# Transposed weight loads in quarters of 1024 columns, and TensorE transposes with filler products at the end of a two-layer recurrent kernel

## The chip, the cores and the metric

The kernel runs on one NeuronCore of a Trainium2 chip. The metric is the device time of one execution in microseconds (us). The engines are TensorE (PE, with its weight loads as PEld), VectorE (DVE), ScalarE (ACT), GpSimd (POOL) and SyncE (SP). SP does no arithmetic here; it issues nearly all DMAs, in program order.

## The reference

A block A (attention in segments, with a carried memory) and a gated block B (GLU) are applied in turn, twice, with the same weights and a layer norm in front of each. All data are bf16.

```python
# x: [1, 2048, 448]; 16 heads of 256; segments of 32 tokens; 8 memory rows
def A(x, mem, Wq, Wk, Wv, Wo):
    for s in range(64):
        h = concat([mem, x[32*s : 32*s+32]])          # 40 rows
        q, k, v = h @ Wq, h @ Wk, h @ Wv              # per head, 448 -> 256
        p = softmax(where(mask, q @ k.T / 16, -1e9))
        o = sum over heads of (p @ v) @ Wo            # 40 x 448
        mem = o[:8]                                   # next segment waits for this
        outs.append(o[8:])
    return concat(outs)
def B(x):                                             # F = 1792
    return (relu(x @ Wg) * (x @ Wu)) @ Wd
x = x + A(ln(x), mem0); x = x + B(ln(x))
x = x + A(ln(x), mem0); x = x + B(ln(x))
```

## The kernel before

**Folded weights.** The kernel first makes, per head, M = Wq Wk^T and N = Wv Wo, both with 448 rows and columns, and keeps them in SBUF (`M`, `M3`, `N`). For this `setup` needs Wq, Wk and Wv with the head dimension on the partitions, so it loads them by transposing DMAs from HBM (`load_t`, issued on SP at line 537), while Wo comes by plain DMAs (`load_o`, line 541). Wq, Wk and Wv are [448, 4096] each; one `load_t` of before moves 2048 columns, that is 1.835 MB, so there are six of them: Wq0, Wk0, Wq1, Wk1, then Wv0, and after two plain loads of Wo (0.92 MB each) Wv1. Then the products: for each of 16 heads three products of two accumulation steps plus a packed fourth for the last 64 rows. The products of four heads (a quarter) are 32 PE instructions, for M as for N, and each result is copied out of PSUM by ACT (line 706) or DVE (line 707). A product waits for the semaphore of the whole DMA that brings its operand: in before, the first eight heads of M wait for Wq0 and Wk0, the other eight for Wq1 and Wk1.

**Steps.** 68 steps `step(t)` follow. Step t works on segment t of layer 0 and on segment t-4 of layer 1. `t_block` forms h M for all heads, `s_mem`, `p_t_mem`, `u_mem`, `un_mem` and `m_t` carry the memory on to the next step, and `s_seg`, `seg_pt`, `u_seg` do the 32 tokens. Two steps make a tile p: `un(p)` multiplies the weighted rows by N (56 pieces), `ln_b(p)` normalizes, `b_layer(p)` is the GLU. In the last step (t = 67) `un(33)`, `ln_b(33)`, `b_layer(33)`, `ln_b(34)` and `b_layer(34)` are called; `b_layer(34)` works on rows that `un(33)` makes, so nothing else is left to run beside the way from `un(33)` to `b_layer(34)`.

**Transposes inside a step.** `seg_pt` turns the softmax weights (`Ps` to `PTs`) and `ln_b` the normalized rows (`xn` to `xBT`) by transposing DMAs from SBUF to SBUF (`tdma`, on SP, line 768). `p_t_mem` turns the small memory part on PE, with the identity matrix as one operand.

**Order of the work.** Operations are recorded with a cost and their reads and writes; `_Order.run` then schedules them on the engines by these costs, due times and the constants of `BIAS`, and hands out the eight PSUM banks (`tile("R", 1)`). The result is a fixed order on each engine; an instruction that waits holds up all that stands behind it on the same engine. In the built program the order of the six `load_t`, four `load_o` and the first two `xAT` transposes (the normalized input rows of the first tiles, from `ln_a`) on SP is: Wq0, Wk0, Wq1, Wk1, Wv0, Wo0, Wo1, Wv1, Wo2, Wo3, xAT, xAT.

Of the kernel before, what the change touches and what calls it, by code (L numbers as in the profile page):

```python
# [6 lines left out]
BF = dt.bfloat16  # L7
# [22 lines left out]
NP = (NSEG + LAG) // 2  # L30
NSTEP = NSEG + LAG
# [346 lines left out]
def MM(out, lhsT, rhs, **kw):  # L378
    return (out, lhsT, rhs, kw)


class _Kernel:
# [131 lines left out]
    def setup(self):  # L514


        S = self
        NW = S.N[:, :, :].rearrange("p o d -> p (o d)")
        BG = S.big[:, :]
        W8 = 8 * D  # L520
# [9 lines left out]
        st = {k: v.rearrange("p (k d) -> p k d", k=8) for k, v in place.items()}  # L530
        src = {"Wq": S.Wq_d, "Wk": S.Wk_d, "Wv": S.Wv_d}

        def load_t(w, i):

            both = {"Wq": NW[:, 4 * i * W8:(4 * i + 2) * W8], "Wk": NW[:, 2 * W8:4 * W8] if i == 0 else BG[:, 0:2 * W8],
                    "Wv": BG[:, (2 * i + 2) * W8:(2 * i + 4) * W8]}[w].rearrange("p (k d) -> p k d", k=16)
            S.q.add("dma", ("sp",), {"sp": 5300.0}, lambda E: E.dma_start_transpose(out=both, in_=src[w][:, i * 2048:(i + 1) * 2048]),
                    (), [(w, 2 * i), (w, 2 * i + 1)], name=f"{w}{i}", lat=2500.0)

        def load_o(q, wr=()):  # L540
            S.q.add("dma", ("sp",), {"sp": 3000.0}, lambda E: E.dma_start(st["Wo", q], S.Wo_d[:, q * 8:q * 8 + 8, :]),
                    (), [("Wo", q)] + list(wr), name=f"Wo{q}", lat=2500.0)
# [1 line left out]
        def small(name, fn, wr, lat=4000.0):  # L544
            S.q.add("dma", ("act",), {"act": 120.0}, fn, (), wr, name=name, lat=lat)

        for i in range(2):
            load_t("Wq", i)
            load_t("Wk", i)
        for p in range(2):  # L550
            S.load_x(p, small)
        small("m0", lambda E: E.dma_start(S.mNc[0:MEM, 0:D], S.mem_d), [("mNc", 0)])
# [35 lines left out]
        T = S.tile("R", 1)  # L588
# [15 lines left out]
        for i in range(H // 2):  # L604
            q = i // 2
            for odd in range(2):
                u = i + 8 * odd
                for kt in range(3):
                    T = S.tile("R", 1)
# [6 lines left out]
            T = S.tile("R", 1)  # L616
            S.mm(lambda T=T, i=i: pair3("Wq", "Wk", i, T), 2 * S.pitch(D), [("Wq", q), ("Wk", q)], T.res() + [("stage",)], mode=6)
            for odd in range(2):
                u, r = i + 8 * odd, slice(64 * odd, 64 * odd + 64)
                for c in range(4):  # L620
                    side, slot = S.PLACE[16 * c + (u if c < 3 else i)]
                    d, w, x = 64 * side, (128 if c < 3 else 64), (64 * odd if c == 3 else 0)
# [4 lines left out]
        S.Nkeys = [("N", o) for o in range(NO)]  # L627

        for q in range(4):
            if q % 2 == 0:  # L630
                load_t("Wv", q // 2)
            load_o(q, [("Wk", q)] if q > 1 else [])
        def n_main(q):
            for h in range(4 * q, 4 * q + 4):
# [126 lines left out]
    def ln_b(self, p):  # L761
        S = self
        S.ln(S.XB[:, p % 2, :], [("XB", p % 2, i) for i in range(3)], 16, "lnB", 1)
        S.tdma("xBT", lambda: S.xBT[:, :, :], lambda: S.xn[:, 1, :], [("xn", 1, 0), ("xn", 1, 1)], [("xBT",)])

    def tdma(self, name, out, src, rd, wr):

        self.q.add("dma", ("sp",), {"sp": 1250.0}, lambda E: E.dma_start_transpose(out=out(), in_=src()), rd, wr, name=name, lat=1150.0)
# [131 lines left out]

    def seg_pt(self, t):
        S = self
        S.tdma("pts", lambda: S.PTs[:, :].rearrange("p (a x) -> p a x", a=4), lambda: S.Ps[:, :, :].rearrange("p a x -> p (a x)"),
               [("Ps",)], [("PTs",)])

# [138 lines left out]
    def un(self, p):  # L1044
        S = self
        O = S.tile("R", 1)
        XA = lambda r, q: S.XA[r, q % 4, :]
        XB = lambda r, q: S.XB[r, q % 2, :]
        lo, x, y = slice(0, 64), slice(64, 96), slice(96, 128)
        if p % 2 and LAG // 2 < p < NSEG // 2:  # L1050

            for k in range(0, NO, 2):
                S.mm(lambda k=k: [MM(O.b()[:, 0:D], S.U[:, o, :], S.N[:, o, :], start=(o == 0), stop=(o == NO - 1)) for o in (k, k + 1)],
                     2 * S.pitch(D), [("U", i, k // 16) for i in range(4)], O.res())
            for src, q, dst, g, half in ((lo, p, lo, p, 0), (x, p - 1, y, p, 1), (y, p, y, p + 1, 1)):
                S.dve(lambda E, src=src, q=q, dst=dst, g=g: E.tensor_tensor(XB(dst, g), O.b()[src, 0:D], XA(dst, q), ALU.add), D,  # L1056
                      O.res(half=(half,)) + [("XA", q % 4, half)], [("XB", g % 2, 2 * half)])
        else:

            u = (2, 3) if p == NSEG // 2 else (0, 1)  # L1060
            for k in range(0, NO, 4):
                S.mm(lambda k=k: [MM(O.b()[64 * (o % 2):64 * (o % 2) + 64, 0:D], S.U[:, o, 32 * u[0]:32 * u[0] + 64], S.N[:, o, :], start=(o < 2), stop=(o >= NO - 2))
                                  for o in range(k, k + 4)], 2 * S.pitch(D), [("U", i, k // 16) for i in u], O.res(), mode=6)
            if p < NSEG // 2:
                S.halves(O, XB(lo, p), XA(lo, p), [("XA", p % 4, 0)], lo, [("XB", p % 2, 0)])
            elif p == NSEG // 2:
                S.halves(O, XB(y, p + 1), XA(y, p), [("XA", p % 4, 1)], y, [("XB", (p + 1) % 2, 2)], 32)
            else:
                r = slice(64, 128)
                S.halves(O, XB(r, p + 1), XA(r, p), [("XA", p % 4, 1)], r, [("XB", (p + 1) % 2, i) for i in (1, 2)])  # L1070
        S.load_x(p + 4)

    def b_layer(self, p):
# [114 lines left out]
```

## Time and profile before

| | us |
|---|---|
| median of 7 runs | 1629.07 |
| lowest, highest | 1624.81, 1632.05 |
| profiled execution, its own time | 1629.28 |
| span of the profile (first to last instruction) | 1627.5 |
| PE busy | 1547.3 (95%) |
| DVE busy | 1070.6 (66%) |
| ACT busy | 718.7 (44%) |
| DMA landing: PTs from Ps, xBT from xn (median) | 2.4, 2.6 |
| mean granted TensorE clock | 0.992 |

The profiled execution took 1.8 us more than its span. It lies 0.2 us above the median. In a line of a timeline the columns are start, duration, engine, source line, operation, output and input, and the count; a bracket at the end gives the idle time of the engine just before and what ended it. In a table of windows PE and PEld are followed by busy us and the number of instructions, and PEclk is the granted clock as a share of full speed.

### The profile page before, as it was taken

To read this page: it belongs to the slowest core of one execution; us is meant where nothing else is said; L and a number is where in the kernel's file an instruction comes from. 1 tells how busy PE (TensorE), PEld (TensorE's weight loads), DVE (VectorE), ACT (ScalarE), POOL (GpSimd) and SP (SyncE) were. 2 spreads that over 40 slices of the span, in tenths; PEclk is the share of its full clock that TensorE was granted. 3 is DMA by queue.
4 is the path that set the end of the run, shared out by engine and by line. 5 is a ranking of instruction groups with operands and counts; after the bars stand their busy time and mean duration, and the time that the engine had idled before them with its cause. 6 is when DMAs were issued, how large, how long until landed. Compare 5 with 4: busy or idle time off the path is not lost. (4 is left out here: it accounts for less than half of the span.)

```text
span 1627.5 us, 67481 instructions
## 1 busy us (share of the span) xinstructions
PE 1547.3 (95%) x30194; PEld 1117.5 (69%) x30194; DVE 1070.6 (66%) x2988; ACT 718.7 (44%) x2163; POOL 90.7 (6%) x156
## 2 busy tenths in 40 slices
PE   4989999999999999999999999999999999999996
PEld 2556767777766776777667776776677777766675
DVE  7746666667666766666666766666667666667554
ACT  4624444445343444444344444444344444534332
POOL 3100000000000000000000000000000000000000
PEclk9989999999999999999999999999999999999999
DMA  9620000000000000000000000000000000000010
GB/s 233 189 84 19 16 14 19 19 15 18 15 19 13 19 16 18 18 14 16 18 16 17 16 19 18 14 15 18 15 17 16 19 19 14 18 13 14 17 21 16
DMA packets 130096, 45.46 MB, mean 28 GB/s; under 512 B 118920, under 2 KB 128912, under 8 KB 129808
## 3 DMA queue, kind: packets, MB, share of 16 engines
q1 hardware_dynamic: 129456, 40.92, 11.4%
q8 instruction: 238, 3.90, 1.0%
q10 hardware_dynamic: 352, 0.24, 0.1%
q14 instruction: 50, 0.41, 0.1%
HBM read 10.33 MB, written 1.84 MB: 7 GB/s over the span
## 5 line engine op out<-in xcount | busy, mean ns | idle before, releaser
L128 PE MATMUL b<-hT,Mw 128*128 128x80 bf16 (+1 forms) x11424 | 440.8, 200 | 12.8 <-DVE big L707 7.3
L128 PEld LDWEIGHTS b<-hT,Mw 128*128 128x128 bf16 x11424 | 418.5, 100 | 35.5 <-DVE big L707 13.3
L128 PE MATMUL b<-Nw,big 128*64 128x448 bf16 (+1 forms) x1936 | 307.7, 356 | 1.4 <-ACT Nw L706 0.7
L128 PE MATMUL b<-xBT,big 128*128 128x128 bf16 (+1 forms) x3920 | 217.9, 217 | 10.0 <-DMA xBT<-xn 10.0
L128 PEld LDWEIGHTS b<-xBT,big 128*128 128x128 bf16 x3920 | 208.0, 99 | 11.6 <-DMA xBT<-xn 11.3
L707 DVE CAST TTs<-b 128x320 bf16<-128x320 f32 (+5 forms) x423 | 192.1, 454 | 32.5 <-PE b L128 31.5
L706 ACT ACTIVATE TTs<-b 64x256 bf16<-64x256 f32 (+4 forms) x461 | 191.7, 416 | 38.9 <-PE b L128 30.8
L128 PEld LDWEIGHTS b<-Nw,big 128*64 128x64 bf16 (+1 forms) x1936 | 126.8, 104 | 111.1 <-issue 19.3
L128 PE MATMUL b<-Nw,UTm 128*32 128x448 bf16 x3752 | 192.3, 356 | 1.4 <-ACT UTm L706 1.3
L706 ACT ACTIVATE TTm<-b 128x80 bf16<-128x80 f32 (+5 forms) x400 | 91.6, 229 | 226.7 <-PE b L128 225.7
L707 DVE CAST TTm<-b 128x80 bf16<-128x80 f32 (+5 forms) x484 | 111.8, 231 | 112.1 <-PE b L128 106.7
L128 PEld LDWEIGHTS b<-Nw,UTm 128*32 128x32 bf16 x3752 | 97.8, 97 | 90.2 <-issue 19.3
L707 POOL COPY hK<-xn 32x448 bf16<-32x448 bf16 x136 | 75.7, 556 | 1462.3 <-DVE xn L743 1456.0
L128 PE MATMUL b<-hT,M 64*128 64x80 bf16 (+3 forms) x3808 | 139.9, 197 | 8.1 <-DVE TTs L707 3.7
L707 DVE CAST big<-b 128x512 bf16<-128x512 f32 (+1 forms) x163 | 107.2, 675 | 58.9 <-PE b L128 57.8
L1090 ACT ACTIVATE gT<-b 128x256 bf16<-128x256 f32 x227 | 85.5, 379 | 106.6 <-PE b L128 81.3
L707 DVE CAST UTm<-b 128x448 bf16<-128x448 f32 (+2 forms) x107 | 64.8, 615 | 101.6 <-PE b L128 100.3
L128 PEld LDWEIGHTS b<-hT,M 64*128 64x128 bf16 (+1 forms) x3808 | 105.7, 97 | 24.3 <-DVE hT L707 10.1
L1091 DVE TENSOR_TENSOR hB<-gT,b 128x256 bf16<-128x256 bf16 x227 | 90.6, 411 | 44.2 <-ACT gT L1090 39.2
L706 ACT ACTIVATE big<-b 128x512 bf16<-128x512 f32 (+1 forms) x225 | 106.4, 514 | 8.1 <-PE b L128 7.0
L950 ACT ACTIVATE hi<-b 128x448 bf16<-128x448 f32 x67 | 36.4, 543 | 146.3 <-PE b L128 144.5
L706 ACT ACTIVATE UTm<-b 128x448 bf16<-128x448 f32 (+2 forms) x144 | 76.3, 552 | 39.5 <-PE b L128 37.6
(100 smaller groups left out, 1520.2 us busy)
## 6 DMA issues: line engine op xcount, KB each, us to landing
big<-in_A_Wo_dram SPq DMA_DIRECT2D x3, 896.0 KB, 5.8
out_dram<-ys SPq DMA_DIRECT2D x32, 56.0 KB, 1.9
big<-in_B_W_down_dram SPq DMA_DIRECT2D x1, 1568.0 KB, 6.9
XA<-in_A_x_dram SPq DMA_DIRECT2D x28, 56.0 KB, 2.2
big<-in_B_W_up_dram SPq DMA_DIRECT2D x1, 1344.0 KB, 5.8
big<-in_B_W_gate_dram SPq DMA_DIRECT2D x1, 1344.0 KB, 8.6
PTs<-Ps SPq DMA_TRANSPOSE x68, 2.4
Nw<-in_A_Wo_dram SPq DMA_DIRECT2D x1, 896.0 KB, 7.5
```

The source lines that it names most:

```text
L128: ins = E.matmul(out, lhsT=lhsT, rhs=rhs, **kw)
L706: return E.activation(out(), src(), ACT.Copy)
L707: return E.tensor_copy(out(), src())
L950: S.act(lambda E: E.activation(S.hi[:, :], C.b()[:, 0:D], ACT.Copy), D, C.res(), [("hi",)])
L1090: S.act(lambda E, k=k, R=R, n=n: E.activation(S.gT[:, k % 2, 0:n], R[0].b()[:, 0:n], ACT.Relu), n, R[0].res(), [("gT", k % 2)])
L1091: S.dve(lambda E, k=k, R=R, n=n, fcs=fcs: E.tensor_tensor(S.hB[:, fcs[0]:fcs[-1] + 1, 0:w], S.gT[:, k % 2, 0:n].rearrange("p (a b) -> p a ...
```

## The change

`load_t` moves 1024 columns (0.92 MB) at a time, so there are twelve of them. SP's order in the built program becomes: Wq0, Wk0, Wq1, Wk1, Wq2, Wk2, Wq3, Wk3, Wv0, Wo0, Wv1, Wo1, Wv2, Wo2, Wv3, Wo3, xAT, the first load of W_up, xAT. A quarter of M or N now waits for the DMAs of its own quarter. On PE the third quarter of N (32 instructions, and two of the fourth) now stands in front of the first `t_block` of step 0, where in before about half of N stood between and behind the parts of that block.

In step 67 `seg_pt` transposes with four PE instructions (`pe_transpose`) and one copy out of PSUM; the built program puts the copy on DVE, between the GLU's products. `ln_b(34)` does the same; its copy is on ACT. After the two additions of `un(33)` that read its PSUM bank, `warm` issues eight products of 512 columns, whose result nobody reads. On PE the order at the end becomes: GLU 33 (112 products, the four transposes of `Ps` after the first 64), weighted rows (5), 2 products of W_down, `un(33)` (56), 12 products of W_down, 8 filler products, 4 transposes of `xn`, GLU 34 (112 and 14). In before, 6 products of W_down stood ahead of `un(33)` and 8 behind it. The instructions of steps 1 to 66 keep their order on every engine.

```diff
-        def load_t(w, i):
-            both = {"Wq": NW[:, 4 * i * W8:(4 * i + 2) * W8], "Wk": NW[:, 2 * W8:4 * W8] if i == 0 else BG[:, 0:2 * W8],
-                    "Wv": BG[:, (2 * i + 2) * W8:(2 * i + 4) * W8]}[w].rearrange("p (k d) -> p k d", k=16)
-            S.q.add("dma", ("sp",), {"sp": 5300.0}, lambda E: E.dma_start_transpose(out=both, in_=src[w][:, i * 2048:(i + 1) * 2048]),
-                    (), [(w, 2 * i), (w, 2 * i + 1)], name=f"{w}{i}", lat=2500.0)
+        def load_t(w, q):
+            S.q.add("dma", ("sp",), {"sp": 3600.0}, lambda E: E.dma_start_transpose(out=st[w, q], in_=src[w][:, q * 1024:(q + 1) * 1024]),
+                    (), [(w, q)], name=f"{w}{q}", lat=2500.0)
...
-        for i in range(2):
-            load_t("Wq", i)
-            load_t("Wk", i)
+        for q in range(4):
+            load_t("Wq", q)
+            load_t("Wk", q)
...
         for q in range(4):
-            if q % 2 == 0:
-                load_t("Wv", q // 2)
+            load_t("Wv", q)
             load_o(q, [("Wk", q)] if q > 1 else [])
...
     def ln_b(self, p):
         S = self
         S.ln(S.XB[:, p % 2, :], [("XB", p % 2, i) for i in range(3)], 16, "lnB", 1)
+        if p == NP:
+            T = S.pe_transpose([("xn", 1, 0), ("xn", 1, 1)], lambda a: S.xn[:, 1, a * 128:a * 128 + 128], [("xBT",)])
+            S.cp(lambda: S.xBT[:, :, :].rearrange("p a b -> p (a b)"), lambda: T.b().bitcast(BF)[:, 0:512], 512, T.res(), [("xBT",)])
+            return
         S.tdma("xBT", lambda: S.xBT[:, :, :], lambda: S.xn[:, 1, :], [("xn", 1, 0), ("xn", 1, 1)], [("xBT",)])
+
+    def pe_transpose(self, rd, src, wr):
+        S = self
+        T = S.tile("R", 1)
+        S.mm(lambda: [MM(T.b().bitcast(BF)[:, a * 128:a * 128 + 128], src(a), S.ident[:, :], is_transpose=True) for a in range(4)],
+             4 * S.pitch(128), rd + [("ident",)], T.res() + wr)
+        return T
+
+    def warm(self, n, rd, wr):
+        S = self
+        T = S.tile("R", 1)
+        S.mm(lambda: [MM(T.b()[:, 0:512], S.ident[:, :], S.N[:, 0:2, 0:256], start=True, stop=True) for _ in range(n)], n * S.pitch(512), rd, T.res() + wr)
...
     def seg_pt(self, t):
         S = self
+        if t == NSTEP - 1:
+            T = S.pe_transpose([("Ps",)], lambda a: S.Ps[:, a, :], [("PTs",)])
+            S.cp(lambda: S.PTs[:, :], lambda: T.b().bitcast(BF)[:, 0:512], 512, T.res(), [("PTs",)])
+            return
         S.tdma("pts", ...)
...
                 S.halves(O, XB(r, p + 1), XA(r, p), [("XA", p % 4, 1)], r, [("XB", (p + 1) % 2, i) for i in (1, 2)])
+                S.warm(8, O.res(), [])
```

## The prediction

> **What bounds the kernel.** I read the page's busy shares first (PE 95%), then the chain of waits, then the timelines of the two ends, since the diff touches only these. Steps 1 to 66 keep their order on all engines, so what an end gains or loses goes whole into the time.
>
> The chain's end:
>
> ```profile
> 1611.16 0.63 DVE part L1041
> ...
> 1613.79 0.19 DVE stat L737
> ...
> 1614.66 0.62 DVE xn L743 x2
> 1615.28 0.02 issue
> 1615.30 2.39 DMA xBT<-xn
> 1617.68 0.05 issue
> 1617.73 6.10 PE b L128 x126
> ```
>
> From the end of `un(33)` at 1611.1 all is serial: two additions, the norm, the transpose by DMA (2.39 us), GLU 34. The granted clock by windows:
>
> ```profile
> 1596.30:1599.00 2.70, 0.70 (x17) 0.56 (x17) 1.84 (x10) 0.67 (x4) 0.00 (x0) 1.00 0.26 55
> ...
> 1600.50:1602.00 1.50, 1.50 (x33) 1.50 (x31) 0.42 (x1) 0.18 (x2) 0.00 (x0) 0.50 0.43 87
> ...
> 1612.00:1617.70 5.70, 0.00 (x0) 0.00 (x0) 3.11 (x7) 0.50 (x2) 0.00 (x0) 0.94 0.15 33
> 1617.70:1619.00 1.30, 1.27 (x24) 1.27 (x25) 0.00 (x0) 0.00 (x0) 0.00 (x0) 0.50 0.00 0
> ...
> 1620.50:1622.30 1.80, 1.80 (x66) 1.75 (x62) 0.48 (x2) 0.75 (x2) 0.00 (x0) 1.00 0.00 0
> ```
>
> After 5.86 us without PE work GLU 34 starts at half clock (0.50), and only from about 1620.3 runs at 1.00.
>
> The beginning, SP's timeline, PE's first products, and the wait at the end of the loads:
>
> ```profile
> 0.74 7.74 SPq L537 DMA_TRANSPOSE Nw<-in_A_Wq_dram  x1
> 8.54 7.79 SPq L537 DMA_TRANSPOSE Nw<-in_A_Wk_dram  x1
> 16.37 7.84 SPq L537 DMA_TRANSPOSE Nw<-in_A_Wq_dram  x1
> 24.26 7.70 SPq L537 DMA_TRANSPOSE big<-in_A_Wk_dram  x1
> ```
> ```profile
> 18.63 13.67 PE L128 MATMUL b<-Nw 128*128 128x448 bf16 x64 [11.40 <-DMA Nw<-in_A_Wk_dram]
> 34.62 11.56 PE L128 MATMUL b<-big,Nw 128*128 128x448 bf16 x64 [2.31 <-issue]
> ...
> 60.49 0.51 PE L128 MATMUL b<-hT,M 64*128 64x40 bf16 x20 [2.57 <-DVE hT L707]
> ```
>
> PE starts when Wk0 is there (18.5), waits 2.31 us for Wk1, and at 57.9 has done all that stands ahead of `t_block`, while xAT, behind ten loads in SP's queue, lands only at 60.2. So the setup ends by the queue, not by its beginning. The DMA rates from 10 to 30 us, in slices of 0.25 us:
>
> ```profile
> GB/s 135 142 178 151 289 278 291 290 289 292 289 288 292 293 287 292 291 290 288 292 291 289 291 292 289 289 292 291 286 294 291 176 85 99 165 289 284 290 257 167
> GB/s 123 0 1 121 267 292 288 290 294 289 287 293 290 290 289 295 288 288 322 271 240 77 8 7 181 277 291 292 288 291 291 159 143 18 146 274 294 289 288 292
> ```
>
> A transpose streams at 290 GB/s, which is 6.33 us for 1.835 MB, yet one is issued every 7.8 us. The 1.45 us between show as dips: about 0.55 us at 17.75, where Wk0 ends and Wq1 begins, then about 0.9, 0.8 and 0.6 us at 19.5, 25 and 28, within 2 us of a data start or end.
>
> **Part 1, the loads.** Six transposes become twelve of half the size. The trace shows no HBM transpose of 1024 columns. Bounds for what each of the six further ones adds: nothing, if the dips go with the bytes; 1.45 us, if all go with the instruction. I take 0.75, a little over the one dip that lies cleanly between two instructions (0.55): 4.5 us. Transposes and copies also alternate more: two more changes from transpose to copy; the rates dip for about 0.6 us at such a change (40.5 to 41.25), so 1.2 us (0 to 1.2). xAT then lands 5.7 us later (0 to 9.9), at 65.9 instead of 60.2. Everything behind it on SP (the loads of W_up, W_down, W_gate, the second xAT) shifts along; these wait for PE's reads of the old weights anyway.
>
> Against this, PE gets its first quarter after two issues of about 4.3 us, half of 7.8 + 0.75, in place of two of 7.8, some 7 us sooner, and M and three quarters of N are done by the time xAT lands. In before, from xAT's use at 60.49 to the product of the memory rows with N at 79.67, PE did half of N (64 instructions) beside `t_block`; now 32 of these lie in front. They are worth 5.5 us: 24 at the pace of N's start (26 in 4.56 us) and 8 in 0.95 us. Setup: 5.7 - 5.5 = +0.2 us; ends -5.5 and +4.4. The moved evictions on DVE and ACT lie beside these products, and both engines idle in the same stretch.
>
> The skill's page "DMA: Bandwidth & Descriptors", section Bandwidth, speaks against this part: it wants DMAs of at least 1 MiB, and a quarter is 0.875 MiB. A line through its rows for 1 MB (6.15 us) and 16 MB (79.0 us) leaves 1.3 us per DMA, an estimate for plain loads; with it the setup would come to +3.5 us in place of +0.2.
>
> **Part 2, the last GLU tile.** *Transpose.* 2.44 us from xn to the first product go. In their place: four PE transposes, 0.23 us for one (`p_t_mem`, at 1582.15) and 0.06 for each further one (128-column products, 32 in 1.95 us), 0.41; the copy of 512 columns on ACT, 0.51 us (mean of that form on line 706); three hand-offs of 0.05. Together 1.07: gain 1.37 us. Bounds: at half clock and with 0.6 for the copy the gain is 0.9.
>
> *Clock.* The eight fillers wait for both additions (1612.4) and PE has 12 products of W_down until about 1612.2. A 512-column product takes about 0.23 us (14 of 448 columns in 2.82 us), so they end at 1614.2, and PE idles 1.0 us until xn and 0.6 us during the copy. The nearest rows: 2.31 us of idle after dense work left the clock at 1.00 (34.6), while 0.8 and 1.3 us with 0.7 us of work between brought 0.50 (1599). Two shorter gaps with 2.2 us of work around them lie nearer to the first, so I take the clock as held. GLU 34's 112 products then go at 27.3 ns (66 in 1.80 us), 3.06 us in place of 4.63: gain 1.57, or 0 if it drops. The fillers stand ahead of nothing but the transposes, which xn releases later.
>
> The skill's page "TensorE: Matmul & The Clock Gate" allows idle gaps up to about 3 us, which would hold the clock, but says in Part 4 that transposes do not count as work. The row at 1599, a drop after gaps of 0.8 and 1.3 us, is stricter than the first rule.
>
> *`seg_pt`.* The DMA of PTs issued at 1599.78 lands 2.4 us later, but PE uses it only at 1604.47: hidden, gains nothing. Its four transposes add 0.3 us to PE ahead of `un(33)` (0.25 to 0.5), the copy 0.68 us to DVE, which idles between the GLU's products. Four products of W_down move behind `un(33)`, 0.5 us off the path. Net -0.2 to +0.3, taken as 0. The 12 behind `un(33)` end near 1612.3, before DVE needs them at 1613.1.
>
> Tail: -1.37 - 1.57 = -2.9 us; ends -3.1 (with -0.2 of `seg_pt`) and -0.6 (0.9 gained, 0.3 lost).
>
> **Sum.** The profiled execution took 1629.28 us; +0.2 - 2.9 gives 1626.6. It lies 0.2 us above the median, so the median becomes 1626.4.
>
> **Rivals.**
>
> (a) *The smaller transposes cost nothing extra* (the dips go with bytes). Setup -5.5, tail -2.9: 1620.7. For it: from 11.4 to 17.7 Wk0 streamed without a dip. Against: the dip at 17.75.
>
> (b) *Every transpose carries its whole 1.45 us.* xAT lands 9.9 us later; setup +4.4, tail -2.9: 1630.6, slower than before. It decides from 1.2 us per extra transpose, where 6 x 1.2 + 1.2 = 8.4 equals the gains of 5.5 and 2.9. For it: four issues within 0.14 us of 7.77.
>
> (c) *The fillers do not hold the clock.* Only the shorter transpose remains, with the setup's +0.2: 1627.9.
>
> (d) *Another stretch at half clock in the setup.* PE now waits between quarters, and a drop like that of 91.3 to 104.8 us (12.2 us busy at 0.50 after a gap of 2.67) costs up to 6 us: 1632.5. For it: that stretch; against: PE waits for loads there anyway.
>
> **How the numbers follow.** Forecast 0.40 (its own range 1624.3 to 1628.6), (a) 0.20, (b) 0.18, (c) 0.12, (d) 0.07, else 0.03. A measurement can tell about 0.2%, 3.3 us, from no change: under 1625.8 is faster, over 1632.3 slower. Faster: (a) and some two fifths of the forecast, 0.36. Slower: most of (d) and a part of (b), 0.11. Same: 0.53. The range from 1621.5 to 1631.0 takes in most of (a) and (b).
>
> **What would show it.** Transpose issues of 4.3 us on SP's timeline, half of 7.8 + 0.75 (3.9 for (a), 4.6 for (b)); xAT in use near 66; the memory product near 80 (74 for (a), 84 for (b)). At the end no DMA of xBT, 1.1 us from xn to the first product, PEclk 1.00 in GLU 34. A product of `un(33)` that waits for the copy of PTs would make Part 2 wrong.

## The result, and the profile after

The changed kernel takes 1622.07 us (median of 14 runs, 1618.27 to 1625.59) against 1628.09 for the kernel before in the same comparison (33 runs); the ratio is 0.9962 with a 95% interval from 0.9952 to 0.9971. That is 6.2 us less (4.7 to 7.8): faster, within the stated range of 1621.5 to 1631.0, but 4.3 us under the number given, and only 0.6 us inside the lower end of the range. Of these 4.3 us, 1.0 is the kernel before: its 33 runs have a median 1.0 us under the 1629.07 from which the number was worked out. The profiled execution took 1623.54 us, 1.8 more than its span of 1621.7.

First the end. The chain of waits of the changed kernel (start, us, engine, output and line):

```profile
1611.43 0.62 DVE xn L739 x2
1612.10 0.41 PE b L128 x4
1612.53 0.60 ACT xBT L702
1613.18 4.91 PE b L128 x126
```

The DMA of 2.39 us is gone; from xn to GLU 34's first product it is 1.13 us. Windows of the same execution, where the number right behind the five engines (PE, PEld, DVE, ACT, POOL) is the granted clock:

```profile
1609.20:1611.20 2.00, 1.90 (x8) 0.70 (x8) 1.87 (x5) 0.39 (x2) 0.00 (x0) 1.00 0.00 0
1611.20:1613.15 1.95, 0.40 (x4) 0.23 (x4) 0.81 (x3) 0.70 (x2) 0.00 (x0) 1.00 0.11 29
1613.15:1616.60 3.45, 3.42 (x114) 3.37 (x116) 0.84 (x2) 1.15 (x3) 0.00 (x0) 1.00 0.02 5
```

Through the eight fillers (first line), the four transposes and GLU 34 the clock stays at 1.00; before, GLU 34 started at 0.50. From GLU 33's first product to the end of the span it is 25.6 us; before it was 28.45 (1599.05 to 1627.5).

Then the beginning, SP's timeline:

```profile
0.75 3.81 SPq L534 DMA_TRANSPOSE Nw<-in_A_Wq_dram  x1
4.61 3.92 SPq L534 DMA_TRANSPOSE Nw<-in_A_Wk_dram  x1
...
28.20 4.03 SPq L534 DMA_TRANSPOSE big<-in_A_Wk_dram  x1
32.27 4.39 SPq L534 DMA_TRANSPOSE big<-in_A_Wv_dram  x1
36.71 0.59 SPq L538 DMA_DIRECT2D big<-in_A_Wo_dram  x1
...
59.55 2.20 SPq L781 DMA_TRANSPOSE xAT<-xn  x1
```

A quarter is issued every 3.9 us, half of 7.8 almost exactly: the last Wk is through at 32.23 us, against 31.96 before, with four transposes more. But xAT, at the end of the queue, is issued at 59.55 instead of 52.85; all but 0.3 of those 6.7 us arise where transposes of Wv and copies of Wo take turns. The DMA rates there, 32 to 60 us in slices of 0.7 us, dip at most changes; the deepest dip, near 35 us, lies between two transposes (Wk3 and Wv0):

```profile
GB/s 290 291 171 143 10 263 291 289 294 114 273 356 338 299 152 290 289 291 244 58 314 335 343 293 97 69 291 290 290 236 94 303 346 300 301 113 191 289 290 291
```

PE's timeline:

```profile
10.77 6.13 PE L128 MATMUL b<-Nw 128*128 128x448 bf16 x18 [4.30 <-DMA Nw<-in_A_Wk_dram]
...
66.77 0.24 PE L128 MATMUL b<-hT,Mw 128*128 128x40 bf16 x3 [0.26 <-DVE hT L703]
...
79.19 2.83 PE L128 MATMUL b<-Nw,UTm 128*32 128x448 bf16 x56 [0.64 <-ACT UTm L702]
```

PE starts 7.9 us sooner, uses xAT 6.3 us later, waits only 0.26 us for it (2.57 before), and reaches the memory product 0.5 us sooner than before (79.67). So far the setup is close to the +0.2 that was predicted. One profile of each kernel was too few to say more; the experiments gave further ones of both setups.

### The profile page after: what moved, and what is told of

Its sections match the earlier page's. It is cut to its first block, busy times and chain, and to the rows that moved or that the text cites. A ratio compares the mean times of both kernels' runs of the same rounds, so it can differ in the third digit from the quotient of the medians.

```text
span 1621.7 us, 67513 instructions
## 1 busy us (share of the span) xinstructions
PE 1550.4 (96%) x30210; PEld 1117.8 (69%) x30210; DVE 1071.4 (66%) x2988; ACT 718.2 (44%) x2165; POOL 90.8 (6%) x156
## 3 DMA queue, kind: packets, MB, share of 16 engines
HBM read 10.33 MB, written 1.84 MB: 8 GB/s over the span
```

## The experiments

Twelve runs in three groups of four; a group shares the runs of the kernel before. The first holds the four below, the second `no_fill`, `pts_dma`, `xat_early` and `pet33`, the third the rest.

### Part 2 alone, Part 1 alone, both, and a regrouped queue

`tail_only` has the loads of before (halves) and the change at the end; `quarters_only` the opposite; `after_again` is the changed kernel once more. `grouped` is the changed kernel with another order of the last eight loads on SP:

```
- Wv0 Wo0 Wv1 Wo1 Wv2 Wo2 Wv3 Wo3 xAT
+ Wv0 Wv1 Wo0 Wo1 Wv2 Wv3 Wo2 Wo3 xAT
```

> The loads of before (six transposes of 2048), and the change at the end (four PE transposes twice, eight fillers). Both theories: the end from GLU 33's first product to the last instruction takes 25.6 us as in the changed kernel, not 28.4, and the whole is 2.9 us faster than before (ratio 0.998). They differ elsewhere: if the 2.2 us that the changed kernel saved between 79 and 107 us are a chance of the clock in two profiles, this kernel may show either value there, and the ratio stays at 0.998; the setup's memory product starts at 79.7 as in before.

> The loads of the changed kernel (twelve transposes of 1024), the end of before. Theory 1 (the parts add, the setup's 0.5 us in the first profile is all it gives, and the 2.2 us of the stretch behind it are chance): ratio 0.9997. Theory 2 (the shorter starved wait of PE and the fewer slow windows at 85 to 107 us follow from the new timing and come back in every run): about 3.2 us faster, ratio 0.998, with the memory product at 79.2 and the first products of the second memory step 24.9 us later, as in the changed kernel, not 27.1.

> The changed kernel once more, beside the others on one chip, for a second profile. The ratio is 0.996 as known. Theory 1: the time from the memory product of step 0 to the selection products of step 1 (24.9 us in the first profile, 27.1 in before) scatters by 2 us between profiles. Theory 2: it is 24.9 again within 0.5.

> The changed kernel with SP's order Wv0 Wv1 Wo0 Wo1 Wv2 Wv3 Wo2 Wo3 in place of Wv0 Wo0 Wv1 Wo1 and so on: still twelve transposes, but as many changes between transposes and copies as in before; PE's order of the last N products moves a little. Theory A (a change between a transpose and a copy costs 1.6 us, a further transpose behind a transpose nothing): xAT is used at 60 to 61 us in place of 66.8, the memory product of step 0 starts 4 to 5 us earlier, at 74 to 75, and the ratio to before is 0.993. Theory B, as predicted (each further transpose 0.75 us, each change 0.6): xAT in use at 65.5, the memory product at 78, ratio 0.9955.

Measured ratios to before: `tail_only` 0.9990 [0.9978, 1.0003], `quarters_only` 0.9979 [0.9966, 0.9991], `after_again` 0.9963 [0.9949, 0.9977], `grouped` 0.9971 [0.9960, 0.9981]. In microseconds of 1627.5 (the median of before there): -1.6, -3.4, -6.0 and -4.7, each with a margin of 1.7 to 2.3. The two parts add up to -5.0, which agrees with -6.0. By its time alone `tail_only` is not clear of no change; what the end is worth is read from the profiles.

The chain of `tail_only`:

```profile
1614.27 0.62 DVE xn L743 x2
1614.93 0.41 PE b L128 x4
1615.37 0.60 ACT xBT L706
1616.02 4.90 PE b L128 x126
```

It is the end of the changed kernel step for step (25.7 us from GLU 33's first product). The chain of `quarters_only` has the old end:

```profile
1609.20 0.62 DVE xn L739 x2
1609.84 2.39 DMA xBT<-xn
1612.28 7.36 PE b L128 x126
```

28.2 us from GLU 33's first product. So in these four profiles the end is worth 2.5 to 2.9 us with either setup. The second profiles, `after_again` and `before_again`, have 26.4 and 29.4 us: one end scatters by about 1 us, and three with the new end lie 2.8 us under three with the old one on the mean.

`grouped` on SP's timeline, and on PE's:

```profile
31.73 9.13 SPq L539 DMA_TRANSPOSE big<-in_A_Wv_dram  x2
...
42.17 11.56 SPq L539 DMA_TRANSPOSE big<-in_A_Wv_dram  x2
53.85 1.14 SPq L543 DMA_DIRECT2D big<-in_A_Wo_dram  x2
55.03 3.54 SPq L786 DMA_TRANSPOSE xAT<-xn  x1
```
```profile
46.56 7.46 PE L128 MATMUL b<-big 128*128 128x448 bf16 x24 [4.48 <-issue]
```

From the last Wk to xAT's issue it takes 23.3 us, in the changed kernel 27.3, in before 20.9. (The other six profiles with quarters have 26.6 to 28.4, the other two with halves 21.1 and 21.7.) `grouped` has four changes of kind, from transposing to copying or back, fewer than the changed kernel with the same transfers: 1.0 us for each change. It has as many changes as before and two more transposes: up to 1.2 us for each. That is one profile of `grouped`. For the queue, Theory A had the place right and the size (1.6) too high. For the time it was wrong: Wo0 now comes later, PE stands 4.48 us ahead of N instead of 0.87, then runs at half clock to about 52 us, and the memory product comes at 79.37. An earlier xAT was paid for with a later N, and by its time `grouped` cannot be told from the changed kernel.

### Each term of the end by itself

`no_fill` leaves the fillers out; `pts_dma` transposes PTs of the last step by DMA again; `pet33` uses TensorE's transposes for GLU 33 too; `xat_early` belongs to the setup and is read below.

```
# no_fill
-                S.warm(8, O.res(), [])
# pts_dma, in seg_pt
-        if t == NSTEP - 1:
+        if False:
# pet33, in ln_b
-        if p == NP:
+        if p >= NP - 1:
```

> The changed kernel without the eight unread products ahead of GLU 34; all else as changed. Theory C (the fillers hold the clock): PE has nothing to do for some 4.9 us but the four transposes, the granted clock falls to 0.50, the 112 products of GLU 34 take about 4.6 us instead of 3.44, from xn to the first product still about 1.1 us; the tail from GLU 33's first product is 1.2 us longer (26.8 instead of 25.6), and the time 1.2 us longer than the changed kernel's. Rival D (the clock in GLU 34 is held by the transposes and the shorter gap alone): 3.4 us, no difference in time.

> The changed kernel, with PTs of the last step transposed by DMA again. As predicted (hidden, taken as 0): the DMA lands about 1.5 us or more before PE's products with PTs, the tail from GLU 33's first product stays at 25.6 us within 0.3, and the time is within 0.3 us of the changed kernel's. Rival: four transposes off PE are worth 0.3 to 0.6 us in GLU 33 and the kernel is that much faster; or PTs comes late and it is over 0.5 us slower.

> The changed kernel, with the transposes of xn on TensorE for GLU 33 too, where the change has them for GLU 34 alone. There the DMA of xBT takes 2.4 us and PE waits 1.56 us for it, and the clock falls to 0.50 for 3.4 us. Theory A (the same two terms as in GLU 34): xn to the first product of GLU 33 in 1.2 us instead of 2.9, gain 1.7, and the clock held, 112 products in 3.1 us instead of 5.0, gain up to 1.7: time 1.7 to 3.4 us shorter than the changed kernel's. Rival B (the work of the last step's softmax, Ps and PTs, is late then and ends the wait before un(33)): gain under 0.7 us, with PE idle ahead of the products with PTs.

Ratios: `no_fill` 0.9968 [0.9949, 0.9987], `pts_dma` 0.9998 [0.9986, 1.0010], `pet33` 0.9976 [0.9965, 0.9987].

`no_fill`, a window in GLU 34 and its products:

```profile
1612.55:1616.00 3.45, 3.42 (x66) 3.42 (x66) 0.42 (x1) 0.38 (x1) 0.00 (x0) 0.52 0.02 5
```
```profile
1612.58 4.99 PE L128 MATMUL b<-xBT,big 128*128 128x64 bf16 x112 [0.69 <-ACT xBT L702]
```

Half clock, 4.99 us instead of 3.44, 27.2 us from GLU 33's first product instead of 25.6: the fillers hold the clock, and GLU 34 alone is 1.55 us longer without them. The timing alone (0.9968 against 0.9962) does not resolve that.

`pts_dma` was the surprise: all of the gain is gone, where nothing was expected. Its timeline:

```profile
1606.05 1.90 PE L128 MATMUL b<-Nw,ident 128*128 128x512 bf16 x8
1607.99 0.62 DVE L1059 TENSOR_TENSOR part<-b,XA 64x448 f32<-64x448 f32 x1 [7.05 <-PE b L128]
...
1613.45 5.33 PE L128 MATMUL b<-xBT,big 128*128 128x64 bf16 x112 [0.69 <-ACT xBT L702]
```

PTs by DMA was not late: PE went into the products with PTs without a wait. What changed is the order that the planner wrote. Without the four transposes it puts twelve of the 14 products of W_down in front of `un(33)`, where the changed kernel has two, and the fillers behind the last two, ahead of the two additions. The fillers are listed as readers of `un(33)`'s accumulator, and the scheduler lets two engines read a PSUM bank only one after the other; so the first addition, on the chain that sets the end, waits for fillers that nobody reads (1607.99, where they end at 1607.95; `un(33)` had ended at 1605.9). Then PE has nothing for 4.2 us and GLU 34 runs at half clock. GLU 33's first product to the end: 30.6 us instead of 25.6.

`pet33` falls into the same hole:

```profile
1603.65 1.90 PE L128 MATMUL b<-Nw,ident 128*128 128x512 bf16 x8
1605.58 0.62 DVE L1059 TENSOR_TENSOR part<-b,XA 64x448 f32<-64x448 f32 x1 [7.05 <-PE b L128]
```

GLU 33 itself gained what Theory A said (its 112 products took 2.97 + 0.63 us where the changed kernel takes 2.96 + 2.04, and no DMA is waited for ahead of them), and the end gave it back.

To show that the order is the cause, `fill_after_add` keeps `pts_dma`'s edit and makes the fillers wait for the second addition:

```
-                S.warm(8, O.res(), [])
+                S.warm(8, [("XB", (p + 1) % 2, 2)], [])
```

> The changed kernel with PTs of the last step by DMA, as pts_dma, but the eight fillers wait for the second addition of un(33) in place of reading its accumulator. In pts_dma they stood right behind un(33), and the first addition began at 1607.99, only when they had ended (1607.95; un(33) itself had ended at 1606.1). Theory A (that order is what pts_dma lost): the first addition starts 0.1 us behind un(33), xn to be transposed 4.2 us behind it instead of 6.0, so the time is at least 1.9 us shorter than pts_dma's (1625.5 or less); GLU 34 at 3.4 us if the clock holds over an idle of 1.3, then 1.0 and 0.6 us (then 1623.7), at 4.6 to 5.3 us if not. Rival B (pts_dma loses by the late PTs itself, or by chance): the same 1627 us, with a wait ahead of the products with PTs.

```profile
1610.66 0.62 DVE L1059 TENSOR_TENSOR part<-b,XA 64x448 f32<-64x448 f32 x1 [5.03 <-PE b L128]
...
1612.00 1.90 PE L128 MATMUL b<-Nw,ident 128*128 128x512 bf16 x8 [1.19 <-DVE XB L1060]
...
1615.90 3.44 PE L128 MATMUL b<-xBT,big 128*128 128x64 bf16 x112 [0.69 <-ACT xBT L702]
```

The first addition goes as soon as `un(33)` ends, GLU 34 is at full clock again, and the end takes 26.5 us, 4.1 less than `pts_dma`. The ratio is 0.9970 [0.9958, 0.9981], clear of `pts_dma`'s. Theory A holds.

### The setup: xAT in front

`xat_early` moves one issue on SP:

```
- ... Wk3 Wv0 Wo0 Wv1 Wo1 Wv2 Wo2 Wv3 Wo3 xAT
+ ... Wk3 xAT Wv0 Wo0 Wv1 Wo1 Wv2 Wo2 Wv3 Wo3
```

> The changed kernel with one edit: on SP, xAT of the first step is issued straight behind Wk3 and not behind Wo3, so it comes in front of the eight Wv and Wo loads; t_block then lies in front of N on PE. Theory A (the queue's order is what the setup loses by: PE idles 6 us between 42 and 67 us, waiting for Wv and Wo, with t_block locked behind xAT): t_block starts near 43, N ends some 2 us after the last Wo quarter (near 68), the memory product is at 72 to 74 instead of 78 to 79, the time 4 to 6 us shorter than the changed kernel's. Rival B (PE's work and the later loads of W_up, W_down and W_gate set the pace): memory product at 77 to 79, or earlier with a wait for those loads behind it; time within 1.5 us of the changed kernel's.

Ratio 0.9949 [0.9933, 0.9964], 1618.39 us. SP's and PE's timelines:

```profile
32.28 1.27 SPq L789 DMA_TRANSPOSE xAT<-xn  x1
```
```profile
43.46 0.54 PE L128 MATMUL b<-hT,M 64*128 64x40 bf16 x30 [1.77 <-DVE M L711]
...
74.05 2.83 PE L128 MATMUL b<-Nw,UTm 128*32 128x448 bf16 x56 [0.81 <-DVE Nw L711]
```

`t_block` fills the time in which PE waited for Wv and Wo, and the memory product comes at 74.05. That is Theory A. Against the changed kernel the time is some 2 us shorter by the ratios, 3.7 by the medians, less than the 4 to 6 expected. Why is not shown. In this profile step 1 is slow behind it (27.3 us from the memory product to step 1's selection with `hi`, 25.1 in the changed kernel), but the seven profiles with the changed kernel's setup have 24.7 to 27.1 us there.

### The parts together, and the idle behind the loads

`best` is the changed kernel with xAT in front, TensorE transposes for GLU 33 too, and 13 fillers that wait for the first addition only. `best_gate` also lets the load of W_gate wait for PTm of step 1:

```
# best
-                S.warm(8, O.res(), [])
+                S.warm(13, [("part", 1)], [])
# best_gate: the two DMAs of W_gate are listed behind p_t_mem of step 1,
# with ("PTm",) as what they read
```

> Candidate for a faster kernel: the changed kernel, with xAT issued behind Wk3 (as xat_early), xn of GLU 33 transposed on TensorE too (as pet33), and 13 fillers that wait for the first addition of un(33) in place of 8 that read its accumulator. Theory A (the parts add): memory product near 74, GLU 33 starts 1.3 us behind the last product of the step with hT instead of 3.1 to 4.2, the first addition 0.1 us behind un(33), fillers from 0.7 to 3.8 us behind it, GLU 34's 112 products in 3.4 us; time 1616 to 1618, 4 to 6 us under the changed kernel. Rival B (13 fillers delay xn's transposes, or the clock drops all the same): GLU 34 at 4.6 us or more, time 1619 to 1621.

> As best, and the load of W_gate, which is first used at 126 us, waits for the memory step of step 1 (PTm, near 92 us) instead of going right behind W_down at 75 us. In all profiles PE idles 1.9 to 2.7 us near 84 to 91 us for no wait that shows, when these loads end and PE's instructions are fetched, and then runs at half clock for 7 to 17 us. Theory A (the loads hold up PE's instructions): the idle goes, the clock stays at 1.00 there, time 2 to 6 us under best. Rival B (the idle has another cause, such as the rate at which t_block uses up instructions): the idle stays at 1.9 us or more, time within 1.5 us of best.

> The kernel before once more, for a second profile of its setup. If the lead of the quarters in the setup is steady: memory product near 79.4 (79.1 to 79.7 so far with halves, 76.5 to 79.2 with quarters), step 1's selection products 24.5 to 27.5 us behind it. If it is chance: memory product anywhere from 76.5 to 79.7.

`best`: 1617.26 us, ratio 0.9927 [0.9913, 0.9940]. `best_gate`: 1616.32 us, ratio 0.9917 [0.9903, 0.9931], 13.5 us (11.2 to 15.8) under before. Both are clear of the changed kernel. `best` on PE's timeline:

```profile
86.35 0.52 PE L128 MATMUL b<-hT,M 64*128 64x40 bf16 x20 [2.71 <-issue]
...
1602.35 2.98 PE L128 MATMUL b<-Nw,ident 128*128 128x512 bf16 x13 [0.53 <-DVE part L1067]
...
1606.25 3.44 PE L128 MATMUL b<-xBT,big 128*128 128x64 bf16 x112 [0.69 <-ACT xBT L710]
```

The two lines at the end show the fillers off the chain and GLU 34 at full clock; GLU 33's first product to the end takes 24.5 us. The first line shows an idle of 2.71 us for which no wait is recorded; every profile with the old W_gate load has one (1.4 to 2.9, 1.86 in the changed kernel). In `best_gate`, SP and then PE at the same place:

```profile
89.74 0.37 SPq L664 DMA_DIRECT2D big<-in_B_W_gate_dram  x1
```
```profile
84.53 0.42 PE L128 MATMUL b<-hT,M 64*128 64x40 bf16 x20
```

With the load moved from 75.5 to 89.7 us the idle is gone, and the granted clock from 84 to 92 us is 0.88 instead of 0.62. All 13 profiles with the early load have the idle, and the one with the late load does not, which points to the load. That PE's instructions came late fits, but the runs don't show it apart. The move also changed the order of some products of `un(0)`, so load and order are not told apart by this one profile. GLU 0 starts 1.8 us sooner than in `best` (123.53 against 125.33); the two times differ by 0.9 us, which the intervals don't separate, less than the 2 to 6 expected.

`before_again` (one run, 1629.33 us) has the memory product at 80.64. With it there are three profiles with halves (`before`, `before_again`, `tail_only`) and seven with quarters and an unchanged order up to the last step (`after`, `after_again`, `quarters_only`, `no_fill`, `pts_dma`, `pet33`, `fill_after_add`). Means, with the ends:

| us from the span's start | halves (3) | quarters (7) | difference |
|---|---|---|---|
| xAT in use on PE | 60.43 (59.77 to 61.03) | 65.60 (64.11 to 66.77) | +5.2 |
| memory product of step 0 | 79.81 (79.11 to 80.64) | 78.02 (76.53 to 79.19) | -1.8 |
| last selection with `hi` | 1588.2 (1587.8 to 1589.1) | 1585.1 (1582.0 to 1588.4) | -3.1 |

## Why the prediction was right or wrong

**The bound and the mechanism.** Right: the end is a serial chain, and the setup ends by a balance of the queue and PE's work. The forecast was "the tail gains, the setup about even". The tail did as forecast or a little better; the setup did better by 2.0 us, and with the 1.0 us by which the kernel before was faster than the base of the forecast this puts the time under the forecast's own range of 1624.3 to 1628.6.

**Tail, -2.9 forecast, -2.85 in the first two profiles.** Transpose: 1.13 us from xn to the first product, 1.1 forecast (the copy took 0.60 on ACT, not 0.51). Clock: held, as the step said, in all five profiles with this end as it is (`after`, `after_again`, `tail_only`, `grouped`, `xat_early`), where GLU 34's 112 products took 3.44 us each time; 3.06 was forecast. With the old end they took 4.63, 5.75 and 5.89 us (`before`, `before_again`, `quarters_only`), because the half clock lasts longer in some executions. So the clock term is 1.2 in the first two profiles and 2.0 on the mean, where 1.57 was forecast; `no_fill` has 1.55. The other 0.3 us of the 2.85 lie ahead of xn, where two profiles of the changed kernel differ by 0.7. So the mechanism is shown, and that -2.85 came so close to -2.9 is in part luck.

**`seg_pt` taken as 0.** Right for the changed kernel, but for a reason that the step did not have. It priced the four transposes and their copy and saw the W_down products move. It did not ask what that move does to the fillers. `pts_dma` measures it: without the transposes the fillers land in front of the additions, and the end loses 5.0 us.

**Part 1, what the extra transposes cost.** The two prices that made up "+5.7 us until xAT" were both wrong in size. A further transpose among transposes costs 0.07 us in the first two profiles (0.27 for four) and 0.2 on the mean (the last Wk is through at 31.1 us with halves, 32.0 with quarters), not 0.75: there rival (a) was nearly right, and its sign, issues of 3.9 us, was seen. Where transposes and copies alternate, a change costs 1.0 us, not 0.6, and a further transpose up to 1.2 (`grouped`), not 0.75; and the sum counted two more changes, from transpose to copy, where there are four, two of them back again. So xAT was issued 6.9 us later on the mean. It was in use only 5.2 us later, 5.7 forecast: the errors cancelled, which is luck. One part of it is seen in the landing of xAT, 7.3 to 8.3 us behind its issue with two copies of Wo right ahead (`before`, `before_again`, `tail_only`, and 7.8 in `grouped`) and 6.9 and 5.6 with one (`after`, `after_again`). For that reason the 74 us of rival (a) did not come: its price held for the loads of Wq and Wk and not for those of Wv.

The Trainium skill's page "DMA: Bandwidth & Descriptors" (section Bandwidth) wants at least 1 MiB in a DMA. Among transposes back to back this case disagrees: with 0.875 MiB each the further DMAs cost 0.07 to 0.2 us apiece, where the estimate from that page's rows, which are for plain loads, was 1.3. Where transposes and copies take turns, a further transpose came to 1.2 us, near that estimate, but the four changes of kind cost more there.

**Part 1, what PE gains.** Here is the step that was off: "worth 5.5 us". From xAT's use to the memory product the three profiles with halves take 19.4 us, the seven with quarters 12.42; the gain is 7.0 us. The missing 1.5 us have two parts. The first is the products of N that no longer stand beside `t_block`. In `before`, then in the changed kernel, without the last eight, which both have at 0.95 us:

```profile
63.75 5.27 PE L128 MATMUL b<-big 128*128 128x448 bf16 x28
71.83 1.05 PE L128 MATMUL b<-big 128*64 128x448 bf16 x6
72.82 4.32 PE L128 MATMUL b<-big 128*128 128x448 bf16 x22
```
```profile
72.25 0.92 PE L128 MATMUL b<-big 128*128 128x448 bf16 x4
73.11 3.57 PE L128 MATMUL b<-big 128*128 128x448 bf16 x18
```

That is 34 products and 6.1 us less. The step counted 32, without the two of the fourth quarter. (Its pace of "26 in 4.56 us" comes from a window that also counts products cut by its ends; the timeline has 24 in that time, and 5.5 is the sum with these 24, while 24 at the written pace would give 5.2.) The second part, 0.9 us on the mean (0.7 in `before`), is the clock. Windows of `before`, then of the changed kernel, behind the use of xAT:

```profile
60.50:62.00 1.50, 1.50 (x52) 1.45 (x53) 1.16 (x5) 0.00 (x0) 0.91 (x2) 0.50 0.06 11
62.00:63.70 1.70, 1.70 (x57) 1.70 (x55) 1.10 (x6) 0.40 (x2) 1.64 (x2) 0.50 0.52 77
```
```profile
66.80:68.50 1.70, 1.70 (x75) 1.63 (x76) 1.04 (x5) 0.30 (x1) 1.15 (x3) 1.00 1.02 403
```

In before PE waits 2.57 us for xAT (4.58 and 3.48 in the other two) and then runs at half clock for 3.3 us (4.3 and 3.4), in which the same 60 products of `t_block` take 2.17 us that take 1.70 in the changed kernel. With quarters PE waits 0.2 to 0.4 us and the clock stays at 1.00. The prediction read the 2.57 us of idle from the profile, but did not look at the clock behind them, though it did exactly that for GLU 34. So the setup came to +5.2 - 7.0 = -1.8, not +0.2.

**Rivals.** (b) failed at its price (1.45 forecast, 0.07 to 1.2 measured). (c) failed; `no_fill` is what it would have been. (d), one more stretch at half clock in the setup, did come, but where it costs little: with quarters the clock is at 0.50 for some us near 20 to 25 us in all seven profiles and between 50 and 56 us in four of them, while PE waits for loads there anyway. The stretch behind xAT, which did cost, went. The one between 80 and 105 us stays, longer or shorter from one execution to the next.

**The sum.** -1.8 for the setup and -2.85 for the tail make -4.65; measured are -6.2 (4.7 to 7.8). With the clock term of the mean the tail is -3.3 (1.3 for the transpose and 2.0) and the sum -5.1, inside the interval. The table's last line leaves another -1.3 between step 0 and the last step, where both kernels have the same instructions in the same order. Its scatter between executions of one order is 6 us, so it may be nothing; its cause stays open. The theory of the first group that fewer slow stretches follow from the new timing was not shown: with the loads of before and with quarters the stretch behind step 0 was seen long and short. The time lies in the part of the range that was there for rival (a), whose price held for a part of the loads only, so the lower end of the range took the measured time in for another reason than the one it was set for.

## What to carry to other kernels

Price a wait with the clock behind it, not only with its length: behind a gap in PE's work, look at the granted clock of the next few windows. When a change is ordered by a planner, ask of each moved instruction who else's place depends on it, and tie filler work to an event that must have happened (here the first addition) rather than to the buffer that the critical chain still reads. Keep transfers of one kind together on a DMA queue, but only as far as the first consumer's data does not come later for it.

## What the runs showed of the hardware that was not expected

- Transposes from HBM of half the size, back to back, are nearly free (issued every 3.9 us for 0.92 MB, every 7.8 for 1.84 MB); a change between transposing and copying on the queue costs about 1.0 us (`grouped` against the changed kernel).
- Fillers of 1.9 us between gaps of 1.2 and 0.9 us keep the clock at 1.00 (`fill_after_add`); 0.7 us of work between gaps of 0.8 and 1.56 us ahead of GLU 33 do not (0.69 from 1595 to 1600 in the changed kernel); nor do four transposes of 0.4 us after 3.1 us without work (`no_fill`).
- The length of a gap alone does not decide. At the start of N's second part, near 50 us, PE idles 2.97 us in `after_again` and the clock stays at 1.00; it idles 2.98 us in `quarters_only` and the clock falls to 0.50. Behind the same wait for xBT in the old end the half clock made GLU 34 take 4.63, 5.75 or 5.89 us.
- PE idles 1.4 to 2.9 us, with no wait recorded, when the load of W_gate streams beside `t_block`, and does not in the one profile in which that load comes later.
- The same order of instructions reached the last selection with `hi`, in the last step, between 1582.0 and 1588.4 us: one profile of each kernel cannot place a difference of 2 us inside a long body.
